# Order of work in VectorE's and ScalarE's queues around six operands of TensorE, in a fused sigmoid attention with two mixtures of experts

## The chip, the cores and the metric

One core of a Trainium2 chip runs the whole program in one launch. The metric is the device time of a run in microseconds (us): the kernel before takes 557.77 us, the median of three runs between 557.51 and 558.12.

## The reference

Three stages follow one another. B = 4 batches of 448 tokens, 12 heads of 64 columns, so x has 1792 rows of 768.

```python
# 1 sigmoid attention, per batch and head
scores = q @ k.T / sqrt(64) - log(448)
x = (1 / (1 + exp(-scores))) @ v                 # laid out as (1792, 768)
# 2 mixture of experts with a skip: 8 experts, w1 (768, 1024), w2 (1024, 768)
do = x @ w_skip > 0
e = argmax(x[do] @ w_gate);  p = softmax value at e
x[do] += p * (relu(x[do] @ w1[e]) @ w2[e])
# 3 mixture of experts on the result: 8 experts, weights of the same shape
logits = (x / |x|) @ (emb / |emb|).T / tau
e = argmax(logits);  p = softmax value at e
out = p * (relu(x @ v1[e]) @ v2[e])
```

The inputs decide which expert takes which token, so the kernel routes at run time: it counts, plans, and branches on the counts.

## The kernel before, in words

**Attention.** 84 steps. Step by step TensorE computes scores into `psS` (L622), ScalarE the sigmoid `A` of them (L626), and TensorE the weighted sum `psO` (L640). Other work rides along: a list `at` (L693) says after which step each piece of it is issued. Six of these pieces cast one sixth of the first dense operand to `xs` on ScalarE (L737).

**Precision.** TensorE multiplies fp32 operands as three products of a rounded ("high") and a remainder ("low") part: `mm3` at L814 to L816. ScalarE makes the high part of a weight (`h`, L804), VectorE the low part by subtraction (`l`, L805). A unit of weights comes in five such pieces: three for the first product (128x512) and two for the second (128x768); `split_unit(u)[:3]` and `split_unit(u)[3:]` are these.

**A dense expert.** `dense()` has eight rounds f. h(f) is 18 matmuls into one of two PSUM banks used in turn ("bank"); ScalarE takes its relu, rounded, `hh` (L834), VectorE the remainder `hl` (L835). Then come the extras `sub(2f)`, then y(f-1), 18 matmuls into the six accumulators `YS`, three for each 128 columns, then `sub(2f+1)`. After the last round y(7) stands alone. `beside(units, steps)` makes `sub`: at number k it issues the weight splits and loads of `units(k)` and the steps filed under k, and those under k - 0.5 ahead of the units of k. Each engine works through its queue strictly in the order in which the program issued to it, so a step's number decides where its instructions stand in every engine's queue.

**The steps that ride in a dense block.** s1 is 24 (or 32) small matmuls of the next routing (L250), copied out by ScalarE (L260); s2 turns two tiles of the result (L267) and VectorE reduces them (`lgs`, L268). Where the second mixture's logits need |x|, `squares_sum()` adds up the squares of the six column tiles on VectorE (L1143, L1145: `row`, `G`), and s1 reads `G`. `add_y(b)` adds the six `YS` of the block just ended to x (L1234), six additions on VectorE.

**An item.** Tokens that are alone with their expert are done as an item: a gather by matmul (L967, whose operand `sel` is built from the plan), h over four quarters of the weights (L1003, relu by ScalarE at L1008), `hT(s)` which turns the relu (two transposes, L1016, and VectorE's copy to `sel`, L1017), and y (L1028), which writes `YS[0]`. `it.hT(1)` is the last of these turns.

**The path that this data takes.** A first dense block in two halves (from 150.4 us), block j=1 of the first mixture with an item (`one_item`, 214.5 to 293 us), then four blocks of the second mixture (j = 0 to 3); the last ends in `finish_last`, which copies the six `YS` to `stg` (L1449 VectorE, L1451 ScalarE, in turn), turns them on TensorE (L1399), scales and stores. `gate_tokens` turns a gate (two small matmuls, L1415) for the blocks of the second mixture.

The program text has other branches (no dense block, no item, many items), which this data does not take.

Of the kernel before, what the change touches and what calls it, by code (L numbers as in the profile page):

```python
# [21 lines left out]
def sigmoid_attention_moe_moe_kernel(  # L22
# [526 lines left out]
    def attention():  # L549


        with ExitStack() as a:
# [112 lines left out]
            for g in range(G + LAG):  # L665
                w, h = divmod(g, NH)
                if 0 < w < N - 2 and h == 0:
                    load_qk(w + 2)
                if g < G:
                    score(w, h)  # L670
                if w + 1 < N and 0 <= h - LAG < 4:
                    load_v(w + 1, h - LAG)
                if w + 1 < N and h in (3, 4):
                    turn(w + 1, "kq"[h - 3])
                for r in {LAG: (), LAG + 1: (LAG + 1, LAG)}.get(h, (LAG,)):
                    if g >= r:
                        av(*divmod(g - r, NH))
                for f in [todo.pop(0)] if todo and g >= 2 else late.get(g, ()):
                    if f:
                        f()  # L680
                done = g - LAG + 1
                if done % NH == 0 and done > 0:
                    b, d = duos[done // NH - 1]
                    if d == NP // 2 - 1 and b < B - 1:
                        assert not todo
                        s1, s2, s3 = route_stages(R1, b, x_of(b))
                        todo = [None, s1, s2, None, s3]
                        if b == B - 2:
                            ge = []
                            fs = [  # L690
                                s1, s2, s3, lambda: ge.append(gates(R1, 0, B - 1)), lambda: ge[0](), lambda: plan_first(R1),
                            ] + first_steps()
                            at = [g + i for i in (2, 3, 5, 5, 7, 8, 10, 10, 12, 13, 15, 16, 17, 18, 19)] + [G]  # L693
                            todo, late = [], schedule({}, fs, at)
            return ST[N - 1, "o"]

# [120 lines left out]

    NF = 2 * NU

    def dense(xs, sub, f0=0, f1=NF, end=None):  # L820

        def h(f):
            h1, l1 = W[f // 2 % 2][:2]
            g = f % 2 * 128
            ps = bank("ps_h")
            for c in range(ND):
                mm3(
                    ps[:, :S], h1[:, c, g : g + 128], l1[:, c, g : g + 128], xs[:, 0, c, :], xs[:, 1, c, :],  # L830
                    c == 0, c == ND - 1,
                )
            a, l = HH[f % 2], HL[f % 2]
            nc.scalar.activation(a, ps[:, :S], AF.Relu)  # L834
            nc.vector.scalar_tensor_tensor(l, ps[:, :S], 0.0, a.bitcast(F32), op0=ALU.max, op1=ALU.subtract)  # L835

        def yc(f, c):
            h2, l2 = W[f // 2 % 2][2:]
            g = f % 2
            mm3(  # L840
                YS[c][:, :S], h2[:, g, c * 128 : c * 128 + 128], l2[:, g, c * 128 : c * 128 + 128],
                HH[f % 2], HL[f % 2], f == 0, f == NF - 1,
            )

        def y(f):
            for c in range(ND):
                yc(f, c)

        for f in range(f0, f1):
            h(f)  # L850
            sub(2 * f)
            if end and f == NF - 1:
                end(yc, lambda: sub(2 * f + 1))
                return
            if f:
                y(f - 1)
            sub(2 * f + 1)
        if f1 == NF:
            y(NF - 1)

    def enumerated(fs):
        return dict(enumerate(fs))
# [318 lines left out]
    def next_dense(j):  # L1181

        box = {}
        xs = XST[(j + 1) % 2]

        def start():
            box["b"], box["e"] = rest_regs(j)
            load1(w1, box["e"], 0)
            load2(w2, box["e"], 0)
            gate_cols(R1, box["b"])  # L1190

        def rows():
            gate_rows(bank("ps_G"))
            box["p"] = split_gated(xs, box["b"])
            for p in range(2):
                box["p"](p)

        def last():
            load_unit(w1, w2, box["e"], 1)
            for f in split_unit(0)[:3]:  # L1200
                f()

        return {
            8: start, 10: rows, 11: lambda: [box["p"](p) for p in (2, 3)], 12: lambda: [box["p"](p) for p in (4, 5, 6)], 13: last,
            14: lambda: [f() for f in split_unit(0)[3:]],
        }

    def units1(e):
        def f(k):
            u, r = k // 4, k % 4  # L1210
            if r == 0 and u + 2 < NU:
                load_unit(w1, w2, e, u + 2)
            if u + 1 < NU and r % 2 == 0:
                for g in split_unit(u + 1)[:3] if r == 0 else split_unit(u + 1)[3:]:
                    g()

        return f
# [54 lines left out]
    def block1(j, before):  # L1272

        b, e = rest_regs(j - 1)
        xs = XST[j % 2]

        def r2():
            if j > 1:
                return {}
            f = route2_steps(0, XST[0])  # L1280
            return at_subs((1, 4, 6, 0, 2, 3, 5, 6, 8), f[:3] + f[5:])

        def general():
            with tc.If(count(R1) > 0) as cmp:
                before()
                it = Item(0, 0)
                at, prep = it.ready(0)
                dense(xs, beside(units1(e), schedule(merge(r2(), at), prep, (3, 3, 7))))
                it.hT(1)()
                add_y(b)  # L1290
                it.finish(start2(j > 1))
            with cmp.Else():
                before()
                dense(xs, beside(units1(e), r2()))
                add_y(b)
                for f in start2(j > 1):
                    f()
                nothing()
            rare()

        def one_item():
            before()
            it = Item(0, 0)
            at, prep = it.ready(0)
            one, two, three = start2(j > 1)
            steps = schedule(merge({12: one, 14: three}, r2(), at), prep, (3, 3, 7))
            dense(xs, beside(units1(e), steps))
            it.hT(1)()
            add_y(b)
            it.finish([two, None, None])  # L1310

        n = 3 * NL[0] + 3 + j
        with tc.If(nc.values_load(R1.LI[0:1, n : n + 1], min_val=0, max_val=NL[0]) < 1, label=f"one{j}") as cmp:
            if j == B - 1:
                general()
            else:
                with tc.If(NB["n"] > j) as more:
                    before()
                    dense(xs, beside(units1(e), merge(r2(), next_dense(j), {13: lambda: likely(f"one{j + 1}")})))
                    block1(j + 1, lambda: add_y(b))  # L1320
                with more.Else():
                    general()
        with cmp.Else():
            one_item()
# [18 lines left out]
    for i in range(2):  # L1343
        take_x(B - 1, NP // 2 - 1, i, last_x[i])

    def rest_of_first():
        for f in split_unit(0)[3:]:
            f()

    rest2 = lambda: at_subs((10, 11, 12, 8, 9, 9, 12, 13, 14, 15, 15), route2_steps(0, XST[1]))  # L1350
    nb_load = lambda: nc.values_load(K["pb"][0:1, 12:13], min_val=0, max_val=B - 1)
    with tc.If(FIRST["n"] < 1, label="none") as cmp:
        rest_of_first()
        run({0: s1, 1: s2, 2: s3, 3: lambda: gates(R1, B - 1, B)(), 4: pl[0], 5: pl[1], 6: pl[2]})
        run(item_steps(R1, (0, 1, 2)))
        run(rest2())
        with tc.If(nb_load() > 0):
            run(next_dense(0))
            b, e = rest_regs(0)
            dense(XST[1], beside(units1(e), {}))  # L1360
            add_y(b)
        leftovers_now(lambda: start2(True))
        rare()
    with cmp.Else():
        b, e = FIRST["b"], FIRST["e"]
        rest_of_first()
        early = {
            0: s1, 2: s2, 4: s3, 5: [pl[0], lambda: gates(R1, B - 1, B)(), lambda: likely("last")], 6: pl[1], 7: pl[2],
        }
        dense(XST[0], beside(units1(e), early), 0, NF // 2)  # L1370
        NB["n"] = nb_load()
# [6 lines left out]
        with cmp2.Else():  # L1378
            steps = merge(
                next_dense(0), item_steps(R1, (9, 11, 13)),  # L1380
                {12: lambda: raw(batch_of(0)), 13: lambda: likely("one1"), 15: squares},
            )
            dense(XST[0], beside(units1(e), steps), NF // 2)
            block1(1, lambda: add_y(b))


    e = expert_of(0)
# [13 lines left out]
    def gate_tokens(j, box):  # L1401
# [14 lines left out]
            t = box["gt"] = sm.tile([128, NK], F32, tag="gtt", name="gtt", bufs=1)  # L1416
            nc.vector.tensor_copy(t, ps[:, :NK])

        return {3: ready, 9: turned}

    def finish(j, b, gt):

# [18 lines left out]
    def finish_last(j, b, it=None):  # L1441
# [3 lines left out]

        def copy(c):
            o = STG[:, c * S : (c + 1) * S]
            if c % 2:
                nc.vector.tensor_copy(o, YS[c][:, :S])  # L1449
            else:  # L1450
                nc.scalar.activation(o, YS[c][:, :S], AF.Copy)  # L1451
# [159 lines left out]
```

## Time and profile before

| | |
|---|---|
| median of 3 runs | 557.77 us |
| the profiled execution | 558.37 us |
| its span, first to last instruction | 556.5 us |
| TensorE matmuls busy | 542.7 us, 98% of the span |
| VectorE busy | 298.9 us, 54% |
| ScalarE busy | 251.9 us, 45% |
| GpSimd busy | 54.0 us, 10% |
| TensorE clock granted, mean | 0.997 |

A row of the timeline gives the start, the busy time, the engine, the line, the operation with the tile it writes and those it reads, the count, and in brackets how long the engine had stood idle before it and what ended that. Matmuls overlap in the pipeline, so a row's busy time is longer than the distance to the next: a full 128x448 matmul follows the last one after 0.20 us though its row says 0.36. The list of waits sums the idle time of TensorE by the line that waited and the line it waited for.

### The profile page before, as it was taken

Reading aid. Unit: us, or ns where it says so; the run is one execution under the profiler, and the core shown is the slowest. Engines: PE = TensorE matmul, PEld = TensorE weight load, DVE = VectorE, ACT = ScalarE, POOL = GpSimd, SP = SyncE. Lnnn points to the kernel's source line nnn. Section 1 sums busy time; section 2 is a strip of 40 time slices with the busy share of each in tenths; the row PEclk is TensorE's granted clock in tenths of the full one; section 3 lists DMA queues with packets and bytes.
Section 4 is the critical chain, followed back from the end, with each engine's and each line's share of the span. In section 5 each row is a group of like instructions: output and inputs, shape, how many; then the busy total and the mean of one; then the engine's idle time right before and its main releaser. Section 6 shows DMA issues by size and latency. Waiting matters only on the chain.

```text
span 556.5 us, 10107 instructions
## 1 busy us (share of the span) xinstructions
PE 542.7 (98%) x3663; PEld 425.3 (76%) x3663; DVE 298.9 (54%) x810; ACT 251.9 (45%) x409; POOL 54.0 (10%) x133
## 2 busy tenths in 40 slices
PE   8999999999999999899999999999999999999995
PEld 5464644545479888699868898999899998989983
DVE  3633445237767677674137677694576545553212
ACT  5766776766943365233208463175233421222112
POOL 5010000000000000165000000040003000305000
PEclk9999999999999999999999999999999999999998
DMA  9868665773460513332737206317624741456353
GB/s 169 147 114 141 115 120 106 133 127 99 167 203 30 171 58 120 114 114 81 260 115 244 96 2 228 113 35 174 191 98 107 200 133 58 138 83 224 114 226 103
DMA packets 169712, 73.34 MB, mean 132 GB/s; under 512 B 134466, under 2 KB 161302, under 8 KB 169632
## 3 DMA queue, kind: packets, MB, share of 16 engines
q1 hardware_dynamic: 147904, 65.94, 44.0%
q10 hardware_dynamic: 21360, 5.97, 4.5%
q0 software_dynamic: 368, 0.53, 0.5%
q8 instruction: 31, 0.51, 0.4%
q14 instruction: 49, 0.40, 0.2%
HBM read 66.90 MB, written 5.60 MB: 130 GB/s over the span
## 4 chain that ended last, share of the span: by engine, by line
PE 91%; DVE 3%; ACT 2%; DMA 1%; issue 1%; DVEq 0%; ACTq 0%
PE bank L814 11%; PE psS L622 11%; PE y L814 10%; PE y L816 10%; PE y L815 10%; PE bank L816 10%; PE bank L815 10%; PE psO L640 10%; PE bank L1003 1%; PE y L1028 1%; ACT A L626 1%; DVE l L805 1%; PE bank L250 1%; DMA k<-in_k_dram 1%; PE ps_r L250 1%
## 5 line engine op out<-in xcount | busy, mean ns | idle before, releaser
L834 ACT ACTIVATE hh<-bank 128x448 fp32r<-128x448 f32 x48 | 26.1, 545 | 194.8 <-PE bank L816 179.2
L814 PE MATMUL bank<-xs,h 128*128 128x448 f32 x288 | 107.1, 372 | 1.6 <-DVE hl L835 1.0
L814 PE MATMUL y<-hh,h 128*128 128x448 f32 x288 | 107.0, 371 | 0.0
L816 PE MATMUL bank<-xs,l 128*128 128x448 f32 x288 | 105.5, 366 | 0.1
L816 PE MATMUL y<-hh,l 128*128 128x448 f32 x288 | 105.5, 366 | 0.0
L815 PE MATMUL y<-hl,h 128*128 128x448 f32 x288 | 105.5, 366 | 0.0
L815 PE MATMUL bank<-xs,h 128*128 128x448 f32 x288 | 105.3, 366 | 0.0
L626 ACT ACTIVATE A<-psS,bias 128x896 f32<-128x896 f32 x84 | 83.3, 1006 | 34.7 <-PE psS L622 34.4
L835 DVE SCALAR_TENSOR_TENSOR hl<-bank,hh 128x448 fp32r<-128x448 f32 x48 | 29.8, 622 | 123.0 <-ACT hh L834 119.8
L805 DVE TENSOR_TENSOR l<-r,h 128x512 fp32r<-128x512 f32 (+1 forms) x115 | 87.5, 809 | 5.1 <-ACT h L804 3.5
L622 PE MATMUL psS<-qT,kT 64*64 64x448 f32 x672 | 87.3, 541 | 0.3 <-ACT A L626 0.3
L640 PE MATMUL psO<-A,v 64*64 64x448 f32 x672 | 86.4, 539 | 0.0
L804 ACT ACTIVATE h<-r 128x512 fp32r<-128x512 f32 (+1 forms) x115 | 74.4, 708 | 0.2 <-issue 0.2
L814 PEld LDWEIGHTS bank<-xs,h 128*128 128x128 f32 x288 | 54.1, 188 | 9.8 <-issue 1.6
L640 PEld LDWEIGHTS psO<-A,v 64*64 64x64 f32 x672 | 34.7, 133 | 32.2 <-issue 20.0
L814 PEld LDWEIGHTS y<-hh,h 128*128 128x128 f32 x288 | 54.1, 188 | 5.6 <-issue 1.2
L816 PEld LDWEIGHTS bank<-xs,l 128*128 128x128 f32 x288 | 54.1, 188 | 4.9 <-DVE l L805 0.4
L815 PEld LDWEIGHTS y<-hl,h 128*128 128x128 f32 x288 | 54.1, 188 | 4.8 <-issue 0.2
L816 PEld LDWEIGHTS y<-hh,l 128*128 128x128 f32 x288 | 54.1, 188 | 4.6
L815 PEld LDWEIGHTS bank<-xs,h 128*128 128x128 f32 x288 | 54.1, 188 | 4.3
L622 PEld LDWEIGHTS psS<-qT,kT 64*64 64x64 f32 x672 | 32.4, 132 | 30.3 <-issue 16.2
L979 POOL COPY row<-xT 128x6 f32 x64 | 18.3, 305 | 212.8 <-PE bank L814 201.0
(269 smaller groups left out, 419.4 us busy)
## 6 DMA issues: line engine op xcount, KB each, us to landing
r<-in_moe_w_dram SPq DMA_DIRECT2D x62, 768.0 KB, 5.2
k<-in_k_dram SPq DMA_DIRECT2D x44, 112.0 KB, 2.9
q<-in_q_dram SPq DMA_DIRECT2D x44, 112.0 KB, 3.2
v<-in_v_dram ACTq DMA_DIRECT2D x44, 112.0 KB, 2.9
out_dram<-row SPq DMA_DIRECT2D x12, 336.0 KB, 3.8
stg<-in_moe_w_dram SPq DMA_DIRECT2D x1, 768.0 KB, 7.7
row<-in_moe_w_dram SPq DMA_DIRECT2D x1, 768.0 KB, 8.9
out_dram<-row SPq DMA_DIRECT2D x1, 672.0 KB, 3.9
```

The lines of the kernel that those rows point to most:

```text
L250: nc.tensor.matmul(ps[q : q + 32, :w], lhsT=lhsT, rhs=tokens(rhs, h), start=first, stop=last)
L622: nc.tensor.matmul(ps[KT * i : KT * i + KT, j, :S], lhsT=kT[r, i, h * KT : (h + 1) * KT], rhs=qT[r, i], start=True, stop=True,)
L626: nc.scalar.activation(at, ps[:, :, :S], AF.Sigmoid, bias=bias, scale=1.0 / math.sqrt(D))
L640: nc.tensor.matmul(ST[w, "o"][i][D * j : D * j + D, :S], lhsT=t[r, j, h, :], rhs=at[r, j, :], start=h == 0, stop=h == NH - 1,)
L804: nc.scalar.activation(dst_h, src, AF.Copy)
L805: nc.vector.tensor_sub(dst_l, src, dst_h.bitcast(F32))
L814: nc.tensor.matmul(ps, lhsT=ah, rhs=bh, start=first, stop=False)
L815: nc.tensor.matmul(ps, lhsT=ah, rhs=bl, start=False, stop=False)
L816: nc.tensor.matmul(ps, lhsT=al, rhs=bh, start=False, stop=last)
L834: nc.scalar.activation(a, ps[:, :S], AF.Relu)
L835: nc.vector.scalar_tensor_tensor(l, ps[:, :S], 0.0, a.bitcast(F32), op0=ALU.max, op1=ALU.subtract)
L979: nc.gpsimd.tensor_copy(self.xb[:, :, t : t + 1], xT[:, :, ds(o, 1)])
```

## The change

All edits are of order but the last, which also cuts one copy in two; the matmuls stay the same in kind and number.

- In attention the list `at` issues the sixth `xs` piece and what goes with it one step earlier, so that each of the last sigmoids but one has a cast ahead of it and one piece, not two, follows the last.
- The first block's `split_unit(0)[3:]` is filed under -0.5 of the dense block instead of being issued ahead of it; its place is now behind `hh` and `hl` of h(0).
- In block j=1 `squares_sum()` is issued before `add_y(b)`, not as step 0 behind h(0), where `f[5]` of the list of steps was that.
- s2 moves to 2.5, and the units' second split moves from remainder 2 to 3 (`half=3`), so `lgs` and the reads that follow stand ahead of the two 128x768 low parts. The item's preparation moves from 3 to 2.5 with it.
- `it.hT(1)` is called inside the last y, after its second column tile (`mid`), instead of after it.
- `next_dense`'s start (the gate's columns for the next block) moves from 8 to 7.5, ahead of the units of 8.
- `gate_tokens` is turned at 8 instead of 9 where j > 0.
- In `finish_last` the copy of the last `YS` is made in two halves, columns 0 to 223 by ScalarE and 224 to 447 by VectorE, instead of whole by VectorE.

```diff
-  at = [g + i for i in (2, 3, 5, 5, 7, 8, 10, 10, 12, 13, 15, 16, 17, 18, 19)] + [G]
+  at = [g + i for i in (2, 3, 5, 5, 7, 8, 10, 10, 12, 13, 14, 15, 16, 17, 18, 19)]
...
-    def dense(xs, sub, f0=0, f1=NF, end=None):
+    def dense(xs, sub, f0=0, f1=NF, end=None, mid=None):
...
         if f1 == NF:
-            y(NF - 1)
+            for c in range(ND):
+                yc(NF - 1, c)
+                if mid and c == 1:
+                    mid()
...
-            8: start, 10: rows, 11: lambda: [box["p"](p) for p in (2, 3)], ...
+            7.5: start, 10: rows, 11: lambda: [box["p"](p) for p in (2, 3)], ...
...
-    def units1(e):
+    def units1(e, half=2):
...
-            if u + 1 < NU and r % 2 == 0:
+            if u + 1 < NU and r in (0, half):
...
-            return at_subs((1, 4, 6, 0, 2, 3, 5, 6, 8), f[:3] + f[5:])
+            return at_subs((1, 4, 6, 2, 2.5, 5, 6, 8), f[:3] + f[6:])
...
-            steps = schedule(merge({12: one, 14: three}, r2(), at), prep, (3, 3, 7))
-            dense(xs, beside(units1(e), steps))
-            it.hT(1)()
+            steps = schedule(merge({12: one, 14: three}, r2(), at), prep, (2.5, 3, 7))
+            dense(xs, beside(units1(e, 3), steps), mid=it.hT(1))
             add_y(b)
...
-        rest_of_first()
         early = {
-            0: s1, 2: s2, 4: s3, ...
+            -0.5: split_unit(0)[3:], 0: s1, 2: s2, 4: s3, ...
...
-            block1(1, lambda: add_y(b))
+            block1(1, lambda: [squares_sum(), add_y(b)])
...
-        return {3: ready, 9: turned}
+        return {3: ready, 8 if j else 9: turned}
...
-            if c % 2:
+            if c == ND - 1:
+                w = S // 2
+                nc.scalar.activation(o[:, :w], YS[c][:, :w], AF.Copy)
+                nc.vector.tensor_copy(o[:, w:], YS[c][:, w:S])
+            elif c % 2:
```

In the changed program lines up to the end of attention stand one lower, those of `dense` where they were, and those of the items and blocks three higher in number (L1016 becomes L1019, L1234 L1237, L1143 L1146).

**VectorE at the start of the first dense block.** The queue behind the branch, before: `l_1760` are the two 128x768 low parts of unit 0, `hl_77` the remainder of h(0).

```order
L1262 UNCONDITIONAL_BRANCH x2
L805 TENSOR_TENSOR l_1760<-r_90,h_1759 128x768 x2
L835 SCALAR_TENSOR_TENSOR hl_77<-bank_1750,hh_75 128x448
L805 TENSOR_TENSOR l_1762<-r_91,h_1761 128x512 x3
L835 SCALAR_TENSOR_TENSOR hl_78<-bank_1750,hh_76 128x448
```

And now:

```order
L1265 UNCONDITIONAL_BRANCH x2
L835 SCALAR_TENSOR_TENSOR hl_77<-bank_1750,hh_75 128x448
L805 TENSOR_TENSOR l_1760<-r_90,h_1759 128x768 x2
L805 TENSOR_TENSOR l_1762<-r_91,h_1761 128x512 x3
L835 SCALAR_TENSOR_TENSOR hl_78<-bank_1750,hh_76 128x448
```

The remainder of h(0) stands ahead of the two low parts; ScalarE's `hh_75` changes places with the two high parts in the same way.

**VectorE at the start of block j=1.** Before, the end of `add_y` (the last `xT`), the remainder of h(0), three low parts, and then `squares_sum` (`row`, `G`, `G`):

```order
L1234 TENSOR_TENSOR xT<-xT,y_1756 128x448
L835 SCALAR_TENSOR_TENSOR hl_77<-bank_1750,hh_75 128x448
L805 TENSOR_TENSOR l_1762<-r_91,h_1761 128x512 x3
L1143 TENSOR_TENSOR row<-row 128x1344
L1145 TENSOR_TENSOR G<-row 128x448
L1145 TENSOR_TENSOR G<-G,row 128x448
L917 TENSOR_LOAD LI_104
```

Now, behind the same branch:

```order
L1265 UNCONDITIONAL_BRANCH x2
L1146 TENSOR_TENSOR row<-row 128x1344
L1148 TENSOR_TENSOR G<-row 128x448
L1148 TENSOR_TENSOR G<-G,row 128x448
L1237 ISA
L1237 TENSOR_TENSOR xT<-xT,y_1751 128x448
```

The three additions of the squares come first, and the six of `add_y`, the remainder and the low parts behind them.

**VectorE around s2 of block j=1.** Before, from the remainder of h(1) on:

```order
L835 SCALAR_TENSOR_TENSOR hl_78<-bank_1749,hh_76 128x448
L805 TENSOR_TENSOR l_1764<-r_92,h_1763 128x768 x2
L268 TENSOR_REDUCE lgs<-bank_1749 112x36
L272 COPY SQ_113<-lgs 112x4
L276 TENSOR_REDUCE t_13942<-lgs 112x4
```

Now:

```order
L835 SCALAR_TENSOR_TENSOR hl_78<-bank_1749,hh_76 128x448
L268 TENSOR_REDUCE lgs<-bank_1749 112x36
L272 COPY SQ_113<-lgs 112x4
L276 TENSOR_REDUCE t_13938<-lgs 112x4
L277 TENSOR_TENSOR SH_105<-lgs,t_13938 112x32
L278 SCALAR_TENSOR_TENSOR d<-SH_105,desc 112x32
L281 TENSOR_REDUCE t_13938<-d 112x4
L288 TENSOR_TENSOR OH_106<-d,t_13938 112x4x8
L973 TENSOR_SCALAR row<-bank_1749 1x64
L805 TENSOR_TENSOR l_1764<-r_92,h_1763 128x768 x2
```

The read of the turned logits, and the small chain behind it, stand ahead of the two low parts of unit 1.

**TensorE at the end of block j=1.** Before, the end of y(7) (`y_1756` is `YS[5]`, `y_1751` is `YS[0]`), hT(1) and the item's y:

```order
L814 MATMUL y_1756<-hh_76,h_1763 128x448
L815 MATMUL y_1756<-hl_78,h_1763 128x448
L816 MATMUL y_1756<-hh_76,l_1764 128x448
L1016 MATMUL bank_1749<-ident,xg_73 128x128 x2
L1028 MATMUL y_1751<-r_89,sel 64x384 x4
```

Now the turn stands between the second and third column tile of y(7):

```order
L814 MATMUL y_1752<-hh_76,h_1763 128x448
L815 MATMUL y_1752<-hl_78,h_1763 128x448
L816 MATMUL y_1752<-hh_76,l_1764 128x448
L1019 MATMUL bank_1749<-ident,xg_73 128x128 x2
L814 MATMUL y_1753<-hh_76,h_1763 128x448
```

Twelve matmuls of y(7) now stand between the transposes and the item's y.

## Rows read from the trace of the kernel before

**Rows 1.** The page, busy time: engine, us (share), instructions.

```profile
PE 542.7 (98%) x3663; PEld 425.3 (76%) x3663; DVE 298.9 (54%) x810; ACT 251.9 (45%) x409; POOL 54.0 (10%) x133
```

**Rows 2.** The list of TensorE's waits: us in total, times, longest.

```profile
PE bank L250 <- DVE G L1145: 1.4, 1, 1.4
...
PE y L1399 <- ACT stg L1451: 0.5, 1, 0.5
PE bank L814 <- ACT h L804: 0.5, 1, 0.5
...
PE bank L814 <- ACT xg L260: 0.2, 1, 0.2
```

**Rows 3.** Timeline of ScalarE, end of attention: start, busy, engine, line, what, count.

```profile
147.31 0.59 ACT L737 ACTIVATE xs<-xg 128x448 fp32r<-128x448 f32 x1
147.78 1.02 ACT L626 ACTIVATE A<-psS,bias 128x896 f32<-128x896 f32 x1
148.69 1.14 ACT L737 ACTIVATE xs<-xg 128x448 fp32r<-128x448 f32 x2
```

**Rows 4.** Timeline of ScalarE, first dense block.

```profile
154.70 0.54 ACT L834 ACTIVATE hh<-bank 128x448 fp32r<-128x448 f32 x1 [0.39 <-PE bank L816]
```

**Rows 5.** Timeline of VectorE, first dense block, first and second half.

```profile
156.25 0.62 DVE L835 SCALAR_TENSOR_TENSOR hl<-bank,hh 128x448 fp32r<-128x448 f32 x1
...
185.34 0.62 DVE L835 SCALAR_TENSOR_TENSOR hl<-bank,hh 128x448 fp32r<-128x448 f32 x1 [2.98 <-ACT h L804]
```

**Rows 6.** Timeline of TensorE, first dense block.

```profile
156.93 0.47 PE L814 MATMUL bank<-xs,h 128*128 128x448 f32 x1 [1.00 <-DVE hl L835]
```

**Rows 7.** Timeline of TensorE: s1 of block j=1, then s1 of a later block.

```profile
221.99 0.96 PE L250 MATMUL bank<-stg,wr 128*32 128x224 f32 x16
...
225.20 0.47 PE L814 MATMUL y<-hh,h 128*128 128x448 f32 x1
...
313.01 0.96 PE L250 MATMUL bank<-stg,wr 128*32 128x224 f32 x16
...
314.66 0.47 PE L814 MATMUL bank<-xs,h 128*128 128x448 f32 x1
```

**Rows 8.** Timeline of VectorE, start of block j=1.

```profile
214.60 3.27 DVE L1234 TENSOR_TENSOR xT<-xT,y 128x448 f32 x6 [2.11 <-PE y L816]
219.05 0.62 DVE L835 SCALAR_TENSOR_TENSOR hl<-bank,hh 128x448 fp32r<-128x448 f32 x1 [1.18 <-ACT hh L834]
...
221.40 1.55 DVE L1143 TENSOR_TENSOR row<-row 128x1344 f32<-128x1344 f32 x1
...
223.64 0.63 DVE L1145 TENSOR_TENSOR G<-G,row 128x448 f32<-128x448 f32 x1
```

**Rows 9.** Timeline of VectorE, s2 of block j=1.

```profile
227.94 0.61 DVE L835 SCALAR_TENSOR_TENSOR hl<-bank,hh 128x448 fp32r<-128x448 f32 x1
...
230.21 0.22 DVE L268 TENSOR_REDUCE lgs<-bank 112x36 f32<-112x72 f32 x1
```

**Rows 10.** Timeline of TensorE, s2 of block j=1.

```profile
228.94 0.38 PE L267 MATMUL bank<-ident,xg 128*112 128x128 f32 x2
230.48 0.61 PE L967 MATMUL bank<-sel,small 112*1 112x64 f32 x8 [1.16 <-DVE lgs L268]
```

**Rows 11.** Timeline of TensorE, end of block j=1.

```profile
286.51 0.38 PE L1016 MATMUL bank<-ident,xg 128*128 128x128 f32 x2
287.94 4.41 PE L1028 MATMUL y<-r,sel 128*64 128x384 f32 x26 [1.04 <-DVE xT L1234]
```

**Rows 12.** Timeline of VectorE, end of block j=1.

```profile
286.93 0.42 DVE L1017 COPY sel<-bank 128x256 f32<-128x256 f32 x1 [7.26 <-PE bank L1016]
```

**Rows 13.** Timeline of VectorE, end of the last block.

```profile
550.18 0.63 DVE L1449 COPY stg<-y 128x448 f32<-128x448 f32 x1 [1.05 <-PE y L816]
```

**Rows 14.** Timeline of TensorE, end of the last block.

```profile
550.86 0.65 PE L1399 MATMUL y<-ident,stg 128*112 128x128 f32 x4 [0.79 <-DVE stg L1449]
```

**Rows 15.** Timeline of ScalarE, s1 of block j=1.

```profile
225.35 0.36 ACT L260 ACTIVATE xg<-bank 128x224 f32<-128x224 f32 x1 [1.19 <-PE bank L250]
```

More of the change, by code (lines that the diff above doesn't have):

```diff
@@ L1203, in next_dense @@
         return {
-            8: start, 10: rows, 11: lambda: [box["p"](p) for p in (2, 3)], 12: lambda: [box["p"](p) for p in (4, 5, 6)], 13: last,
+            7.5: start, 10: rows, 11: lambda: [box["p"](p) for p in (2, 3)], 12: lambda: [box["p"](p) for p in (4, 5, 6)], 13: last,
             14: lambda: [f() for f in split_unit(0)[3:]],
         }
-    def units1(e):
+    def units1(e, half=2):
         def f(k):
@@ L1287, in general @@
                 at, prep = it.ready(0)
-                dense(xs, beside(units1(e), schedule(merge(r2(), at), prep, (3, 3, 7))))
-                it.hT(1)()
+                dense(xs, beside(units1(e, 3), schedule(merge(r2(), at), prep, (2.5, 3, 7))), mid=it.hT(1))
                 add_y(b)
@@ L1293, in general @@
                 before()
-                dense(xs, beside(units1(e), r2()))
+                dense(xs, beside(units1(e, 3), r2()))
                 add_y(b)
@@ L1305, in one_item @@
             one, two, three = start2(j > 1)
-            steps = schedule(merge({12: one, 14: three}, r2(), at), prep, (3, 3, 7))
-            dense(xs, beside(units1(e), steps))
-            it.hT(1)()
+            steps = schedule(merge({12: one, 14: three}, r2(), at), prep, (2.5, 3, 7))
+            dense(xs, beside(units1(e, 3), steps), mid=it.hT(1))
             add_y(b)
@@ L1318, in block1 @@
                     before()
-                    dense(xs, beside(units1(e), merge(r2(), next_dense(j), {13: lambda: likely(f"one{j + 1}")})))
+                    dense(xs, beside(units1(e, 3), merge(r2(), next_dense(j), {13: lambda: likely(f"one{j + 1}")})))
                     block1(j + 1, lambda: add_y(b))
@@ L1344, in sigmoid_attention_moe_moe_kernel @@
         take_x(B - 1, NP // 2 - 1, i, last_x[i])
-    def rest_of_first():
-        for f in split_unit(0)[3:]:
-            f()
     rest2 = lambda: at_subs((10, 11, 12, 8, 9, 9, 12, 13, 14, 15, 15), route2_steps(0, XST[1]))
@@ L1352, in sigmoid_attention_moe_moe_kernel @@
     with tc.If(FIRST["n"] < 1, label="none") as cmp:
-        rest_of_first()
-        run({0: s1, 1: s2, 2: s3, 3: lambda: gates(R1, B - 1, B)(), 4: pl[0], 5: pl[1], 6: pl[2]})
+        run({-1: split_unit(0)[3:], 0: s1, 1: s2, 2: s3, 3: lambda: gates(R1, B - 1, B)(), 4: pl[0], 5: pl[1], 6: pl[2]})
         run(item_steps(R1, (0, 1, 2)))
@@ L1365, in sigmoid_attention_moe_moe_kernel @@
         b, e = FIRST["b"], FIRST["e"]
-        rest_of_first()
         early = {
-            0: s1, 2: s2, 4: s3, 5: [pl[0], lambda: gates(R1, B - 1, B)(), lambda: likely("last")], 6: pl[1], 7: pl[2],
+            -0.5: split_unit(0)[3:], 0: s1, 2: s2, 4: s3, 5: [pl[0], lambda: gates(R1, B - 1, B)(), lambda: likely("last")], 6: pl[1], 7: pl[2],
         }
```

## The prediction

> **What bounds the kernel now.** The page's busy times come first: TensorE's matmuls fill 98% of the span, VectorE 54%, ScalarE 45% [rows 1]. So only two things shorten the run: fewer matmul slots, which this change does not touch, or less of TensorE's idle time. That is why the list of TensorE's waits is read next. It is short: no entry reaches 1.5 us, and every one occurs once, so each belongs to a single place in the program and can be looked up in the timeline [rows 2]. Those that stand there as a row with brackets are h(1) waiting 1.00 for `hl` in the first dense block [rows 6], the item's gather waiting 1.16 for `lgs` [rows 10], the item's y waiting 1.04 for `add_y` [rows 11], and the last turn waiting 0.79 for VectorE's copy [rows 14]; the other four are in the list alone [rows 2]. The reader is to see that a wait's price is TensorE's idle time, and that it ends when one VectorE or ScalarE instruction ends; what matters is what stood ahead of that instruction in its queue.
>
> **The change part by part.**
>
> *End of attention.* ScalarE's queue ends with a sigmoid (147.78), two `xs` casts of 1.14 together, then `h`, for which TensorE waits 0.5 [rows 3, 2]. A cast after the last sigmoid costs 1.14/2 = 0.57; one ahead of a sigmoid costs 147.78 - 147.31 = 0.47. Moving one from the one place to the other brings `h` forward by 0.57 - 0.47 = **0.10**. The last sigmoid itself comes 0.47 later. The weighted sums behind it may slip by at most that, and TensorE idles 0.5 there anyhow, so the idle time covers the slip; without that cover it would cost 0.47 less the 0.10. Bounds -0.4 to 0.1; I take 0.10, since the cover is in the list.
>
> *First dense block.* VectorE's two 128x768 low parts stand ahead of the remainder of h(0). `hl` starts at 156.25 and TensorE follows at 156.93, 0.68 behind [rows 5, 6]. ScalarE's `hh`, which `hl` needs, starts at 154.70 and takes 0.54 [rows 4], so with nothing ahead `hl` starts at about 155.25 and TensorE at 155.93: 156.93 - 155.93 = **1.00**, the whole wait. The low parts that are passed over are wanted only by y(0), which comes after the 18 matmuls of h(1), 18 x 0.20 = 3.6 us later; they and the three behind them fit in.
>
> *squares_sum ahead of add_y.* s1 of block j=1 takes 225.20 - 221.99 = 3.21, the same step elsewhere 314.66 - 313.01 = 1.65 [rows 7]. The difference, **1.56**, is the wait for `G` with its refill [rows 2]. The squares take 224.27 - 221.40 = 2.87 on VectorE [rows 8]. Put first, they run from about 214.4 to 217.3, far ahead of 221.99. What is late next is what they now push: `add_y` (3.27) and `hl` of h(0). 214.60 + 2.87 + 3.27 + 0.62 = 221.36 for the end of that `hl`, against s1 at 221.99, which reuses its bank: 0.6 us to spare. So VectorE's idle 1.18 ahead of `hl` [rows 8] pays for most of the move. Bounds: nothing (all handed on) to 1.56; I take 1.56, since the sum of durations fits.
>
> *s2 and the units.* The item's gather waits 1.16 for `lgs`, which starts at 230.21, behind `hl` at 227.94 and the two low parts [rows 9, 10]. Moved ahead of them, `lgs` waits only for the two transposes, which start at 228.94. VectorE's read behind another pair of transposes starts 286.93 - 286.51 = 0.42 after them [rows 11, 12], and the gather follows `lgs` by 230.48 - 230.21 = 0.27. So the gather starts at 228.94 + 0.42 + 0.27 = 229.63, not 230.48: **0.85**. This needs `hl` of h(1) out of the way in time, since the transposes reuse its bank: TensorE arrives at 228.94 - 1.56 = 227.38. `hl` ended at 227.94 + 0.61 = 228.55; the idle 1.18 which the move fills brings it to 227.37. That is no slack at all by this reckoning, and it is the weakest joint of the sum. Bounds: 0 to 1.16.
>
> *hT(1) inside the last y.* The item's y waits 1.04 for the first addition of `add_y`, because that stands on VectorE behind the copy to `sel`, and the copy behind the transposes at 286.51 [rows 11, 12]. With the turn after six of the 18 matmuls, the copy is done twelve matmuls, some 2.4 us, before the item's y, and `YS[0]` is complete by then too, so its addition runs in that time. The transposes cost TensorE the same in either place. **1.04**. If the relu were late the transposes would stall instead; ScalarE's item work then sits before them with y(7)'s first six matmuls as cover. Bounds 0.5 to 1.1.
>
> *Gate turned at 8.* One wait of 0.2 on `xg` is in reach [rows 2]; I take half, **0.10**, bounds 0 to 0.2. `next_dense` and the other renumbered steps move VectorE work that no wait in the list names: nothing, hidden by the y rounds.
>
> *The last copy in halves.* VectorE's whole copy takes 0.63 from 550.18, TensorE follows at 550.86 [rows 13, 14]. ScalarE moves 128x224 in 0.36 [rows 15], VectorE 128x256 in 0.42 [rows 12]. The two halves read one PSUM bank, and the built order makes VectorE's wait for ScalarE's: first half at 550.54, so the first two transposes start 0.63 - 0.36 = 0.27 earlier, but the later two wait for 550.18 + 0.36 + 0.42 = 550.96 and a hand-over of 0.05, as from the whole copy's end at 550.81 to 550.86: 551.01. They now start half-way through the row of four, at 550.86 + 0.65/2 = 551.19, so they gain 0.18, and the later two decide. I take **0.15**; bounds -0.1 to 0.27.
>
> The Trainium skill, in "PSUM — Partial Sum Buffer", section "PSUM bank collisions raise a hardware error", says that two engines must not read the same bank and partition quadrant at once, so such accesses have to be put in order. No row here shows two engines on one bank at once. By the rule the halves can't overlap and 0.15 stands; without it both halves would be done after 0.42 and the term would be about 0.2.
>
> *Sum.* 0.10 + 1.00 + 1.56 + 0.85 + 1.04 + 0.10 + 0.15 = 4.80. Against the profiled execution, 558.37 - 4.80 = 553.57. That execution is 558.37 - 557.77 = 0.60 above the median, so the median to expect is **553.0 us**.
>
> **The rivals.**
>
> *VectorE hands it back in block j=1.* VectorE does the same work in another order; if its `hl` of h(0) or h(1) comes late, TensorE waits there. For it: the slack of 0 just worked out, and VectorE's idle 2.11 ahead of `add_y` at the block's start, which may not shrink [rows 8]. Against it: 0.6 to spare at s1. Price: from 0.7 to both terms together, 1.56 + 0.85 = 2.41. Time 553.7 to 555.4. Chance 0.23.
>
> *Nothing, or only a trace.* The waits are passed on one after another, or the order built is not that of the text. For it: all seven places are single events. Against it: the queues as built show the moves, and each removed wait has cover worked out above. 557.8 within 1.1. Chance 0.07.
>
> *Slower.* TensorE loses its place in the instruction stream at a branch. VectorE stands idle 2.98 ahead of `hl` at 185.34 and 2.11 ahead of `add_y` at 214.60, both just behind a branch on counts [rows 5, 8]; TensorE passes the same branches with no entry in its list [rows 2]. The changed program has its instructions at other addresses. If two of TensorE's branches paid 2.98 each, 5.96 - 4.80 = 1.16 would be lost: 558.9. It decides from a loss of 4.8 in all, that is 2.4 each. Chance 0.05.
>
> The Trainium skill, in "Runtime: NRT & Kernel Launch", section "Instruction fetch mechanics", says that a taken branch to outside the prefetched window stalls the engine until the target's page has come. VectorE's rows agree with a stall of 2 to 3 us, but don't show its cause; by the rule TensorE could get one where code moves across a page.
>
> **How the numbers follow.** The forecast has 0.62, the first rival 0.23, no change 0.07, slower 0.05, and 0.03 for a gain above the range. All upper bounds together are 0.10 + 1.00 + 1.56 + 1.16 + 1.10 + 0.20 + 0.27 = 5.39, so 552.4; with a little for the median's own spread the low end is 552.0. The first rival's end is 555.4, so the high end is 555.5. About 0.2% (1.1 us) is what a measurement of this kernel tells from no change. Faster: 0.62 + 0.23 + 0.03 = 0.88; same 0.07; slower 0.05.
>
> **What would show it.** In the changed kernel's list of TensorE's waits the entries L250 on `G`, L1028 (now L1031) on `xT` and the first L814 on `hl` are gone; the gather's wait on `lgs` is about 0.3; `h` still ends attention with 0.4. s1 of block j=1 takes 1.65. VectorE's `hl` of h(1) ends before the transposes of s2 begin; if a new entry L267 on `hl` stands in the list, the first rival holds. The last turn's wait shrinks to about 0.5, and a second one may stand within it. The forecast is wrong if TensorE's idle time goes down by less than 3.5 us, or if a stretch behind a branch shows TensorE idle for over 1 us with no engine named.

## The result, and the profile after

The changed kernel takes 552.86 us (median of 4 runs, 552.03 to 553.05) against 557.94 for the kernel before beside it: 5.08 us less, a ratio of 0.9907 (95% interval 0.989 to 0.9924). The forecast was 553.0. The profiled execution takes 553.05, its span is 551.2.

The page's busy times, to set beside [rows 1]:

```profile
PE 542.9 (98%) x3663; PEld 425.3 (77%) x3663; DVE 298.4 (54%) x810; ACT 252.4 (46%) x410; POOL 54.8 (10%) x133
```

Nothing was removed from any engine; ScalarE has one instruction more, the half copy. What changed is the list of TensorE's waits, to set beside [rows 2] (us in total, times, longest):

```profile
PE busy L658 <- POOL ident masks.py:199: 1.4, 1, 1.4
PE y L1394 <- ACT stg L1450: 0.5, 1, 0.5
PE y L1394 <- ACT stg L1445: 0.5, 1, 0.5
PE ps_G L724 <- DVE G L718: 0.4, 1, 0.4
PE psS L622 <- ACT A L626: 0.3, 1, 0.3
PE bank L970 <- DVE lgs L268: 0.3, 1, 0.3
PE bank L816 <- DVE l L805: 0.2, 1, 0.2
```

The four entries of 1.0 us and more that the change was predicted to touch are gone or down to 0.3; the 1.4 at the top is the program's start, as before. The 0.5 for `h` at the first dense matmul is gone as well, where the prediction expected 0.4 to stay. One entry is new: the third matmul of the first dense block waits 0.2 for a low part.

TensorE's timeline, first the start of the first dense block, then s1 and s2 of block j=1 (to set beside [rows 6, 7, 10]):

```profile
150.31 0.48 PE L814 MATMUL bank<-xs,h 128*128 128x448 f32 x1
...
151.18 0.47 PE L816 MATMUL bank<-xs,l 128*128 128x448 f32 x1 [0.19 <-DVE l L805]
...
156.00 0.47 PE L814 MATMUL bank<-xs,h 128*128 128x448 f32 x1
...
221.04 0.96 PE L250 MATMUL bank<-stg,wr 128*32 128x224 f32 x16
...
222.69 0.47 PE L814 MATMUL y<-hh,h 128*128 128x448 f32 x1
...
226.44 0.38 PE L267 MATMUL bank<-ident,xg 128*112 128x128 f32 x2
227.14 0.61 PE L970 MATMUL bank<-sel,small 112*1 112x64 f32 x8 [0.33 <-DVE lgs L268]
```

s1 takes 222.69 - 221.04 = 1.65, as predicted, and the gather follows the transposes by 0.70 where it took 1.54. VectorE in the same block (beside [rows 8, 9]):

```profile
213.63 1.56 DVE L1146 TENSOR_TENSOR row<-row 128x1344 f32<-128x1344 f32 x1 [2.09 <-issue]
...
216.43 3.27 DVE L1237 TENSOR_TENSOR xT<-xT,y 128x448 f32 x6
219.61 0.62 DVE L835 SCALAR_TENSOR_TENSOR hl<-bank,hh 128x448 fp32r<-128x448 f32 x1
220.15 1.89 DVE L805 TENSOR_TENSOR l<-r,h 128x512 fp32r<-128x512 f32 x3
221.95 0.16 DVE L943 TENSOR_SCALAR small<-POS 112x4 f32 x1
...
224.22 0.62 DVE L835 SCALAR_TENSOR_TENSOR hl<-bank,hh 128x448 fp32r<-128x448 f32 x1
226.86 0.23 DVE L268 TENSOR_REDUCE lgs<-bank 112x36 f32<-112x72 f32 x1 [2.02 <-PE bank L267]
```

The reader is to see two things. The remainder of h(0) ends at 220.23, 0.81 ahead of s1. And the remainder of h(1) ends at 224.84, 1.6 us ahead of the transposes at 226.44; VectorE then stands idle for 2.02. The prediction had no slack at all there.

The end of block j=1 on TensorE, and VectorE's answer (beside [rows 11, 12]):

```profile
280.76 0.38 PE L1019 MATMUL bank<-ident,xg 128*128 128x128 f32 x2
...
283.50 2.80 PE L1031 MATMUL y<-r,sel 128*64 128x384 f32 x16
```

```profile
281.18 0.42 DVE L1020 COPY sel<-bank 128x256 f32<-128x256 f32 x1 [4.83 <-PE bank L1019]
281.52 3.27 DVE L1237 TENSOR_TENSOR xT<-xT,y 128x448 f32 x6
```

The copy is done 1.9 us before the item's y, which no longer waits. The last turn, now behind ScalarE's half (beside [rows 14]):

```profile
545.81 0.85 PE L1394 MATMUL y<-ident,stg 128*112 128x128 f32 x4 [0.51 <-ACT stg L1445]
```

Stretch by stretch, with the two times in TensorE's timeline that each is taken from (the tail ends with the span):

| stretch | before | after | gain | predicted |
|---|---|---|---|---|
| first score to h(1) of the first dense block | 148.70 (8.23 to 156.93) | 147.90 (8.10 to 156.00) | 0.80 | 1.10 |
| h(0) to h(2) of block j=1 (squares, s2) | 16.47 (214.55 to 231.02) | 14.07 (213.61 to 227.68) | 2.40 | 2.41 |
| last h to the next block, block j=1 (the turn) | 20.94 (272.31 to 293.25) | 19.82 (268.99 to 288.81) | 1.12 | 1.04 |
| the round with the second gate | 9.60 (384.37 to 393.97) | 9.28 (379.93 to 389.21) | 0.32 | 0.10 |
| last h to the end of the last matmul | 18.76 (532.75 to 551.51) | 18.69 (527.97 to 546.66) | 0.07 | 0.15 |
| last matmul to the end of the span | 5.02 (551.51 to 556.53) | 4.58 (546.66 to 551.24) | 0.44 | none |

The first five make 4.71, of 4.72 between first score and last matmul, so nothing is left there for the renumbered steps that were not tried alone; with the sixth 5.15. The start (first score at 8.23 before, 8.10 after) gives the last 0.13 of the 5.29 by which the two spans differ. That start varies from execution to execution, from 6.89 to 8.23 in the fourteen profiles of this study, so below the stretches decide and the times confirm. Ratios are to the kernel before; the changed kernel's 0.9907 is what they are to be compared with.

### The profile page after: what moved, and what is told of

It reads as the page before. It is cut to its first block, busy times and chain, and to the rows that moved or that the text cites. A ratio compares the mean times of both kernels' runs of the same rounds, so it can differ in the third digit from the quotient of the medians.

```text
span 551.2 us, 10110 instructions
## 1 busy us (share of the span) xinstructions
PE 542.9 (98%) x3663; PEld 425.3 (77%) x3663; DVE 298.4 (54%) x810; ACT 252.4 (46%) x410; POOL 54.8 (10%) x133
## 4 chain that ended last, share of the span: by engine, by line
PE 96%; DVE 1%; ACT 1%; issue 0%; DVEq 0%; POOL 0%; POOLq 0%; ACTq 0%
PE psS L622 11%; PE bank L814 11%; PE y L814 11%; PE psO L640 11%; PE bank L816 11%; PE y L816 11%; PE y L815 11%; PE bank L815 11%; PE bank L1006 1%; PE y L1031 1%; PE bank L250 1%; PE busy L658 1%; PE ps_r L250 1%; ACT A L626 1%; PE ps_t L598 0%; PE y L1394 0%
```

## The experiments

**Squares put back** in the changed kernel.

```diff
-            block1(1, lambda: [squares_sum(), add_y(b)])
+            block1(1, lambda: add_y(b))
-            return at_subs((1, 4, 6, 2, 2.5, 5, 6, 8), f[:3] + f[6:])
+            return at_subs((1, 4, 6, 0, 2, 2.5, 5, 6, 8), f[:3] + f[5:])
```

> The changed kernel with squares_sum put back behind h(0) of block j=1; all other edits stay. Theory (each wait is TensorE idle time of its own): s1 of that block takes 3.2 us again instead of 1.65, with a wait of 1.4 for G, and the time is 1.56 above the changed kernel's 552.9: 554.4. The gather's wait for lgs stays at 0.3, since lgs still stands ahead of the two low parts. Rival (the order of VectorE's queue couples the places): hl of h(1) is late too, the transposes of s2 wait, and the loss is 2.4: 555.3.

553.94 us, ratio 0.9932 (0.9918 to 0.9945). h(0) to h(2) of block j=1 takes 15.63, that is 1.56 more. The list of waits:

```profile
PE bank L250 <- DVE G L1148: 1.4, 1, 1.4
...
PE bank L970 <- DVE lgs L268: 0.3, 1, 0.3
```

The theory held: the wait for `G` is back and the gather's is not. VectorE's timeline shows a second thing, the idle time behind the squares, which the kernel before has as well:

```profile
221.87 0.62 DVE L1148 TENSOR_TENSOR G<-G,row 128x448 f32<-128x448 f32 x1
223.89 0.17 DVE L943 TENSOR_SCALAR small<-POS 112x4 f32 x1 [1.39 <-issue]
```

Between the squares and the item's preparation VectorE stands 1.39 without a releaser, at the loads of plan numbers into registers (the TENSOR_LOAD rows of the order). In the changed kernel the same L943 follows the low parts with no idle time at all. The rows of the first of these loads, in this kernel and then in the changed one, show where the time goes ("x2": it comes twice; the first start is the one here):

```profile
L920 DVEq TENSOR_LOAD <-LI x2: 319/324/330, 221.9 to 483.0; - x2
```

```profile
L920 DVEq TENSOR_LOAD <-LI x2: 319/326/332, 219.7 to 482.1; - x2
```

In this kernel the loads start with the last addition of the squares (221.87), and L943 follows 2.0 behind. Only that addition's 0.62 runs beside them; the rest is the 1.39. In the changed kernel they start with the remainder of h(0) (219.61), and VectorE still has that and three low parts to work through until L943 at 221.95, 2.3 us, which hides them.

**s2 put back** in the changed kernel.

```diff
-            steps = schedule(merge({12: one, 14: three}, r2(), at), prep, (2.5, 3, 7))
-            dense(xs, beside(units1(e, 3), steps), mid=it.hT(1))
+            steps = schedule(merge({12: one, 14: three}, r2(), at), prep, (3, 3, 7))
+            dense(xs, beside(units1(e), steps), mid=it.hT(1))
```

with s2 at 3 in `at_subs`, and the same in the branches that this data does not take.

> The changed kernel with s2 back at 3, the item's preparation at 3 and the units' second split back at remainder 2, so that lgs stands behind the two low parts again. By the sum of the prediction this costs 0.85: 553.7, with a gather that waits 1.16 for lgs. Rival, read from the trace of the changed kernel: there VectorE has finished hl of h(1) at 224.84 and then stands idle for 2.02 until the transposes; the two low parts (1.81) fit into that idle time, so lgs is not delayed: cost 0 to 0.1, gather's wait still 0.3, 552.9. That would mean that the move of the squares alone had already brought this term.

552.69 us, ratio 0.9912 (0.9897 to 0.9927); h(0) to h(2) 14.07, as in the changed kernel to the hundredth. VectorE:

```profile
223.58 0.62 DVE L835 SCALAR_TENSOR_TENSOR hl<-bank,hh 128x448 fp32r<-128x448 f32 x1
224.11 1.81 DVE L805 TENSOR_TENSOR l<-r,h 128x768 fp32r<-128x768 f32 x2
226.23 0.23 DVE L268 TENSOR_REDUCE lgs<-bank 112x36 f32<-112x72 f32 x1 [0.31 <-PE bank L267]
```

The rival held. The two low parts are done 0.31 before `lgs` could start. With the squares moved, the edit on s2 is worth nothing.

**Squares alone, and s2 alone,** on the kernel before.

```diff
-            block1(1, lambda: add_y(b))
+            block1(1, lambda: [squares_sum(), add_y(b)])
-            return at_subs((1, 4, 6, 0, 2, 3, 5, 6, 8), f[:3] + f[5:])
+            return at_subs((1, 4, 6, 2, 3, 5, 6, 8), f[:3] + f[6:])
```

> The kernel before with one edit alone: squares_sum ahead of add_y in block j=1. By the sum of the prediction 1.56 less than before: 556.4, with the gather's wait for lgs left at 1.2. Rival (this move alone also brings VectorE so far ahead that the two low parts are done before the transposes of s2): the gather's wait falls to 0.3 as well, and the gain is 1.56 + 0.85 = 2.4: 555.5.

555.30 us, ratio 0.9954 (0.9941 to 0.9968): 2.8 less than before. The rival held; s2 on TensorE:

```profile
225.87 0.38 PE L267 MATMUL bank<-ident,xg 128*112 128x128 f32 x2
226.57 0.61 PE L967 MATMUL bank<-sel,small 112*1 112x64 f32 x8 [0.33 <-DVE lgs L268]
```

```diff
-            if u + 1 < NU and r % 2 == 0:
+            if u + 1 < NU and r in (0, half):
...
-            steps = schedule(merge({12: one, 14: three}, r2(), at), prep, (3, 3, 7))
-            dense(xs, beside(units1(e), steps))
+            steps = schedule(merge({12: one, 14: three}, r2(), at), prep, (2.5, 3, 7))
+            dense(xs, beside(units1(e, 3), steps))
```

> The kernel before with one edit alone: s2 and the item's preparation at 2.5 and the units' second split at 3 in the block with the item, so that lgs stands ahead of the two low parts. Theory (either of two edits is enough for the gather): VectorE is late in this block as squares_sum is still behind h(0), so here the edit has its full worth: the gather's wait for lgs falls from 1.16 to about 0.3, 0.85 less than before: 557.1 against 557.9; the wait of 1.4 for G stays. Rival (the edit never has any worth): wait 1.16, no change in time.

556.99 us, ratio 0.9984 (0.9975 to 0.9993). Its gather, with `lgs` ahead of low parts that are late here:

```profile
228.64 0.38 PE L267 MATMUL bank<-ident,xg 128*112 128x128 f32 x2
229.35 0.61 PE L967 MATMUL bank<-sel,small 112*1 112x64 f32 x8 [0.33 <-DVE lgs L268]
```

The theory held. The four kernels make a square, h(0) to h(2) of block j=1: 16.47 with neither edit, 15.64 with s2 alone (214.24 to 229.88), 14.08 with the squares alone (213.03 to 227.11), 14.07 with both. s2 is worth 0.83 alone and 0.01 behind the squares; the squares 2.39 alone and 1.57 behind s2.

**One and two more additions on VectorE** in the changed kernel, between the squares and `add_y`, to find where VectorE begins to set the pace. Their results are not used.

```diff
+    def more():
+        n = ND // 2
+        for _ in range(1):     # 2 in the second kernel
+            nc.vector.tensor_add(SQ[:, n:], SQ[:, :n], SQ[:, n:])
...
-            block1(1, lambda: [squares_sum(), add_y(b)])
+            block1(1, lambda: [squares_sum(), more(), add_y(b)])
```

> The changed kernel with one more addition of 128x1344 on VectorE (1.56, its result is not used) between squares_sum and add_y. From the trace of the changed kernel: hl of h(0) ends at 220.23 and s1, which reuses its bank, starts at 221.04: slack 0.75, so s1 waits 0.8 for hl; hl of h(1) ends 1.6 ahead of the transposes, no wait there. Time 0.8 above the changed kernel: 553.7. Rival, the prediction's own reckoning (0.6 to spare at s1, none at hl of h(1)): 0.95 at s1 and a new wait of the transposes for hl of h(1) of about 0.6: 554.4.

> The same with two such additions (3.1 more on VectorE, results not used). Slack 0.75 at s1: s1 waits 2.35, time 555.2, every further us on VectorE costs TensorE one. Rival (VectorE is not what sets s1): less than 1 us, 553.8.

552.75 us, ratio 0.9907 (0.9892 to 0.9922), and 554.53, 0.9937 (0.9923 to 0.995). s1 on TensorE with one:

```profile
220.50 0.96 PE L250 MATMUL bank<-stg,wr 128*32 128x224 f32 x16 [0.41 <-DVE hl L835]
```

and with two:

```profile
222.88 0.96 PE L250 MATMUL bank<-stg,wr 128*32 128x224 f32 x16 [1.96 <-DVE hl L835]
```

h(0) to h(2) grows by 0.48 (212.59 to 227.14) and 2.05 (213.41 to 229.53). The first time does not show its 0.48, or the 0.8 that was expected; the rows decide. Both waits are 0.4 shorter than expected, half of it because VectorE came earlier from its idle time behind the branch: 1.86 and 1.81 before the squares, 2.09 in the changed kernel. The step from one to two is 1.57 for about 1.55 of work, so beyond the first 1.1 us VectorE costs TensorE us for us. And hl of h(1) held nobody up in either. So the first rival's mechanism exists, and the changed kernel stands 0.8 to 1.1 us away from it (its own slack at s1, and the part of the first addition that was free), at s1 alone.

**The turn put back.**

```diff
-            dense(xs, beside(units1(e, 3), steps), mid=it.hT(1))
+            dense(xs, beside(units1(e, 3), steps))
+            it.hT(1)()
```

> The changed kernel with the item's last turn put back behind the last y of block j=1. Theory: the item's y waits 1.04 for the first addition of add_y again, and the time is 1.0 to 1.1 above the changed kernel: 553.9. Rival: the wait had gone for another reason (VectorE earlier in that block), and nothing is lost: 552.9.

553.80 us, ratio 0.9929 (0.9916 to 0.9943). The wait is back at its old size, and last h to the item's y is 1.12 longer; the theory held:

```profile
284.65 2.80 PE L1031 MATMUL y<-r,sel 128*64 128x384 f32 x16 [1.04 <-DVE xT L1237]
```

**The first low parts put back,** and **the casts of attention put back.**

```diff
-            -0.5: split_unit(0)[3:], 0: s1, 2: s2, ...
+            0: s1, 2: s2, ...                 # and issued ahead of dense() again
```

> The changed kernel with the first block's two high and low parts issued ahead of the dense block again. Theory: h(1) of the first dense block waits 1.0 for hl, time 553.9; the new wait of 0.2 within h(0) for a low part stays, since it comes from the end of attention. Rival: the 0.2 came with this edit and goes, so the net loss is 0.8: 553.7.

```diff
-  at = [g + i for i in (..., 12, 13, 14, 15, 16, 17, 18, 19)]
+  at = [g + i for i in (..., 12, 13, 15, 16, 17, 18, 19)] + [G]
```

> The changed kernel with the six xs pieces of attention back on their old steps. By the prediction 0.10 more, with a wait of 0.5 for h at the first dense matmul. By the trace of the changed kernel the first dense matmul came 0.09 earlier but the third waited 0.2 for a low part; so the stretch from the last sigmoid to h(1) should be the same within 0.1, and the wait for h (0.5) takes the place of the wait for l (0.2): 552.9.

Without the first edit: 552.93 us, ratio 0.9915 (0.9901 to 0.9928), less than either expectation and a loss that the time cannot tell from none. But TensorE's row shows it, and h(0) to h(1) takes 6.53 again, not 5.69, so the edit is worth 0.84:

```profile
150.85 0.47 PE L816 MATMUL bank<-xs,l 128*128 128x448 f32 x1 [0.20 <-DVE l L805]
...
156.51 0.47 PE L814 MATMUL bank<-xs,h 128*128 128x448 f32 x1 [0.86 <-DVE hl L835]
```

Without the second: 552.23 us, ratio 0.99 (0.9885 to 0.9916), not distinguishable from the changed kernel. Its only wait there:

```profile
149.79 0.47 PE L814 MATMUL bank<-xs,h 128*128 128x448 f32 x1 [0.49 <-ACT h L804]
```

The wait for `h` (0.5) has returned and that for `l` is gone; first score to h(1) takes 147.84, against 147.90 in the changed kernel. The new wait of 0.2 belongs to the casts, as the theory had it for both kernels, and the edit on the casts is worth nothing. (It moves all six casts one step earlier each, not the sixth alone.) VectorE shows why, first in the kernel before and then in the changed one:

```profile
150.40 1.89 DVE L805 TENSOR_TENSOR l<-r,h 128x512 fp32r<-128x512 f32 x3
```

```profile
149.77 0.62 DVE L738 TENSOR_TENSOR xs<-xg,xs 128x448 fp32r<-128x448 f32 x1 [0.73 <-ACT xs L737]
150.44 1.90 DVE L805 TENSOR_TENSOR l<-r,h 128x512 fp32r<-128x512 f32 x3
```

The first low part stands behind the remainder of the last cast (L738), and that cast comes no earlier: counted from the first score it starts at 141.05, before at 141.02. Counted in the same way, the third matmul of the dense block starts at 142.91 to 143.02 in the four profiles with the old order of the casts and at 143.06 to 143.29 in the ten with the new one. So the edit loses about 0.1 there, if anything.

**The gate put back.**

```diff
-        return {3: ready, 8 if j else 9: turned}
+        return {3: ready, 9: turned}
```

> The changed kernel with the gate turned at 9 again. By the prediction 0.10 more; by the two traces the stretch from s1 to the next h in the second block of the last stage shrank from 2.20 to 1.65, at a price of about 0.2 where the gate went: 0.3 more, 553.2, with the wait of 0.2 on xg back. Below what the time itself can tell; the rows decide.

553.05 us, ratio 0.9919 (0.9905 to 0.9932), no difference that the time can tell. The rows from s1 on:

```profile
386.48 0.96 PE L250 MATMUL bank<-stg,wr 128*32 128x224 f32 x16
...
388.13 0.39 PE L1410 MATMUL bank<-off,sel 112*128 112x14 f32 x2
388.68 0.48 PE L814 MATMUL bank<-xs,h 128*128 128x448 f32 x1 [0.15 <-ACT xg L260]
```

From s1 to the next h it is 2.20 here and 1.65 in the changed kernel, and the round takes 9.61 against 9.28: 0.33, of which the wait is less than half.

**The whole copy put back.**

```diff
-            if c == ND - 1:
-                w = S // 2
-                nc.scalar.activation(o[:, :w], YS[c][:, :w], AF.Copy)
-                nc.vector.tensor_copy(o[:, w:], YS[c][:, w:S])
-            elif c % 2:
+            if c % 2:
```

> The changed kernel with the last copy whole on VectorE again. The prediction gave the halves 0.15; the traces give 0.26 at the first turn but only 0.06 at the scaling behind the last one, since VectorE's half waits for ScalarE's. Theory: the rows behind the last turn come 0.06 to 0.1 later, time 552.9 to 553.0. Rival: the full 0.26 counts, 553.1.

552.96 us, ratio 0.991 (0.9897 to 0.9924), again too close for the time to decide. Last h to last matmul 18.77 against 18.69: 0.08, as the theory had it. But from the last matmul to the end of the span it is 5.03 again, as in the three other profiles with the whole copy (5.01 to 5.04); in the ten with the halves it is 4.57 to 4.64. The last turn:

```profile
544.95 0.65 PE L1394 MATMUL y<-ident,stg 128*112 128x128 f32 x4 [0.79 <-DVE stg L1444]
```

**A step further:** another order of the places into which the last block turns its fourth and fifth column.

```diff
-        place = {0: BANKS + YS[1:3], 3: YS[3:5] + BANKS, 5: [YS[1], YS[2]]}
+        place = {0: BANKS + YS[1:3], 3: [YS[3]] + BANKS + [YS[4]], 5: [YS[1], YS[2]]}
```

> The changed kernel, further: in the last block the four turned token tiles of columns 4 and 5 go to YS[3], the two banks and YS[4] in this order, not YS[3], YS[4], the banks. The second transpose waited 0.53 for ScalarE's copy of YS[4], since it writes where that copy reads; now two transposes more (0.14 each) run ahead of that wait. Theory: the wait falls to about 0.25 and what follows comes 0.28 earlier: 552.6. Rival: the banks are not yet read out by the scaling of the first three columns, and the wait only changes its name: 552.9.

552.72 us, ratio 0.9906 (0.9891 to 0.9921): faster than the kernel before, and not told apart from the changed kernel by the time. Last h to the start of the last transpose takes 18.19, 0.23 less than the changed kernel's 18.42, close to the 0.28 of the theory. The wait that was 0.53:

```profile
539.96 0.43 PE L1394 MATMUL y<-ident,stg 128*112 128x128 f32 x2 [0.31 <-ACT stg L1450]
```

## Why the prediction was right, point by point

- *The bound.* Right: between first score and last matmul TensorE's idle time fell from 7.28 to 2.37, by 4.91 (the prediction's own limit was 3.5), while its busy time rose from 536.00 to 536.19; together that is the gain of 4.72. The largest terms sit where the list of waits had them.
- *End of attention, 0.10.* Wrong by its whole size: 0.0, or a loss of about 0.1. The step that failed is the one from "brings `h` forward by 0.57 - 0.47" to a gain of TensorE. In the timeline `h` starts 0.11 earlier (149.62, before 149.73), but the first score is 0.13 earlier too; counted from there, `h` starts at 141.52 (before 141.50) and the first dense matmul at 142.21 (before 142.17). The wait for `h` is gone because the weighted sums, which slipped with the last sigmoid, now run up to that matmul. And the sum left out the low parts: they stand behind VectorE's remainder of the last cast, which comes no earlier, and the third matmul waits 0.19 for the first of them.
- *First dense block, 1.00.* 0.84, in the changed kernel and again when undone (with a wait of 0.86): the wait went as worked out. Most of the difference is the 0.2 of the step above, which falls into the same stretch: with the casts put back h(0) to h(1) takes 5.57, which is 0.96 less than before.
- *Squares, 1.56, and s2, 0.85.* The sum was right, 2.40 of 2.41; its division was not. The step that failed is "`hl` ... no slack at all by this reckoning". It let VectorE move forward only by the idle 1.18 ahead of `hl`, and left out the second idle time, 1.4 at the register loads behind the squares. It is there in the kernel before (1.40) and with the squares put back (1.39), and not where the loads run beside the remainder of h(0) and the low parts. Why the loads start only with the last addition of the squares, though they are free to start ahead of three low parts, was not tried. With both idle times gone VectorE is ahead by 1.6 at the transposes, the low parts fit in, and the gather's wait goes without the edit made for it. Either edit is enough for the 0.83, and the sum was right because the prediction counted it once.
- *The turn, 1.04.* 1.12, and all of it lost when undone.
- *The gate, 0.10.* 0.32: mis-sized, and above its bound of 0.2. It was bounded by the wait of 0.2, but s1 to h shrank by 0.55 as the two small matmuls and the wait left that place, and they cost about 0.2 where they went.
- *The halves, 0.15.* 0.07 to 0.08 up to the last matmul. The first turn gains 0.27 and the later two wait for VectorE's half, which waits for ScalarE's; the two halves are 0.36 and 0.39, serial, as predicted. The step that was mis-sized is "half-way through the row of four": before, the third of the four transposes stood 0.27 behind the first, not 0.33, and the fourth 0.11 behind the third. Now the fourth follows only 0.16 after the third, which has waited. So the gain is 0.12 at the third and 0.07 at the fourth. Another 0.44 comes behind the last matmul, which no term had. Its cause is open.
- *The rivals.* VectorE handing it back: shown by the added additions to lie 0.8 to 1.1 us away. No change: refuted. Slower by a stall of TensorE at a branch: no such entry; VectorE's idle time behind the branch at block j=1 is still there, 2.09 with no releaser. The other stall that this rival was priced from, 2.98 ahead of `hl` at 185.34, was read too large: ScalarE's `hh`, which that `hl` needs, ran from 183.68 to 184.23, so only the last 1.1 of it can be laid to the branch.

The terms that were too large (0.10 and 0.16 at the start, 0.08 at the end) and too small (0.08 at the turn, 0.22 at the gate, and the 0.44 that was not there at all) partly cancel. That the forecast of 553.0 came within 0.2 us is in part luck; that the gain lies where the waits were is not.

## What to carry to other kernels

Where one engine is 98% busy, its list of waits is a price list, but the items are not always independent: two waits on the same queue can have one cure. Before adding terms, replay the queue behind the first edit and see whether the second wait still has a reason. An idle time without a releaser in front of a waited-for instruction belongs in that replay too, since it may be hidden work that moves with its neighbour.

## What the runs showed of the hardware

- VectorE stands 1.7 to 2.1 us idle behind the branch into block j=1 with no releaser, in all eleven profiles in which the squares come next (1.68 to 2.14). TensorE passes there without a gap. That the branch is the cause was not tried.
- Loads of numbers into VectorE's registers cost it nothing while it still had 2.3 us of work queued ahead of the instruction that needs them, and 1.39 to 1.40 where they started with one addition left.
- The span's end came about 0.4 earlier behind the last matmul in all ten profiles with the copy in halves (4.57 to 4.64) than in all four with it whole (5.01 to 5.04). In the trace 0.33 of it lies between two of GpSimd's closing semaphores (0.41 apart in the whole-copy kernel, 0.08 in the changed one), after the last store has landed. What GpSimd waits for there was not tried, and the median times of the two kernels (552.96 and 552.86) don't show it.
- From the start of the span to the first score it took 6.89 to 8.23 us in fourteen profiles. This range of 1.34 is wider than what any single edit here is worth but the move of the squares, so such edits are told apart by rows and not by one time, and times in two timelines are compared from the first score on.
